# Two attention-plus-spectral layers: row sums directly behind a chunk's last product with V, and all range maxima of weights at chunk boundaries

## The chip, the cores and the metric

The kernel runs on one core of a Trainium2 chip. The metric is the device time of one execution in microseconds (us). A core has a TensorE (PE in the profile, PEld for its weight loads), a VectorE (DVE), a ScalarE (ACT), a GpSimd (POOL) and a SyncE (SP), which issues nearly all DMAs here. Each engine works off its own list of instructions in the listed order; an instruction that waits holds up everything listed behind it on the same engine.

## The reference

The input x is 2048 x 1024. Four residual blocks follow each other: attention, spectral filter, attention, spectral filter, both attentions with the same weights and both filters with the same weights.

```python
def _A_ref(x, wqkv, wo):          # 32 heads of 32
    q, k, v = split(x @ wqkv)
    p = softmax(q @ k.T * Dh ** -0.5)
    return (p @ v) @ wo
def _B_ref(x, w_r, w_i):
    return irfft2(rfft2(x) * (w_r + 1j * w_i))
x = x + _A_ref(_layernorm(x), A_wqkv, A_wo)
x = x + _B_ref(_layernorm(x), B_w_r, B_w_i)
x = x + _A_ref(_layernorm(x), A_wqkv, A_wo)
x = x + _B_ref(_layernorm(x), B_w_r, B_w_i)
```

## The kernel before, in words

"Layer one" is the first attention and the first filter (layer 0 in the code), "layer two" the second pair.

**Range flags.** The fast code represents float32 numbers as pairs of float16, which is exact enough only if the weights lie in a certain range. So the kernel also finds the largest absolute value of all weights, and at the very end `combine_flags` chooses whether a general fallback runs (it doesn't for these inputs). The maxima are VectorE reductions, all in layer one: 48 over the staged pieces of wqkv in `Weights.prep` (L259, 128x512 float32 each), 16 over the pieces of wo that `spectral` loads for that purpose alone (L789), and 32 over the spectral weights in `loadw` (L840). In layer two the same code runs with `flag`/`flags` None and without any of them.

**Start of a layer.** `ln` normalizes 16 tiles of 128 rows, splits each into high and low float16 halves `hl` (L168 on VectorE) and transposes them by DMA into `xh`, `xl` (the tile `big`). Between the tiles TensorE makes the first K, Q and V (L338, L382). `bank()` gives them the PSUM banks o and x in turn; `split` (L167 on ScalarE, L168 on VectorE) empties a bank.

**Attention.** 8 groups of 4 heads (g), each in 4 chunks of 512 queries (c), each in 16 steps of 128 keys (kt): 512 steps per layer. In a step TensorE makes the scores `S` (L564) into two of three PSUM buffers `s`, ScalarE takes the exponentials `p` (L568), and after every second step the products with V, `PV` (L574), follow for two steps together. VectorE adds the exponentials of the chunk into `acc` (`add`, L585 for the first two steps together, L587 for the others). Behind the last `add` of a chunk comes `fin`: four matmuls of `acc` with ones (L593) make the row sums, into an `s` buffer as well; VectorE transposes them (L594), inverts them (L596), spreads them (L599) and scales the chunk's output (L600). `out` writes it to DRAM a few steps later (L607, L609). Every odd step has a slot for "filler" matmuls: K, Q and V of coming groups (L338, L382) in groups 0 to 6, the output projection (L440) in group 7. K and Q fillers use the one x bank, which must be emptied before the next of them starts. `Weights.prep` splits the weights of a coming phase in such slots.

**Order.** In the attention loop the orders of TensorE and ScalarE are as the program is written (`manual_schedule`); those of VectorE, GpSimd and SP come from a list scheduler. In the loop before the change, step 0 of a chunk holds S, then the last two PVs of the chunk before and the add of its step 14; step 1 holds S, the add of step 15 and `fin`.

**Spectral filter.** `spectral` transforms along one axis (`t1`, `fa`), then runs a loop of 36 turns over 32 units (`fb`, `fc`, `binv`, `cinv`: transform, multiply with a weight tile `w` of `loadw`, transform back), then the last transform (`t2`, `ai`). In `loadw` GpSimd changes signs in the tile `w` (L848), behind the reduction of the same tile.

Of the kernel before, what the change touches and what calls it, by code (L numbers as in the profile page):

```python
# [6 lines left out]
F32 = mybir.dt.float32  # L7
# [5 lines left out]
ALU = mybir.AluOpType  # L13
AX = mybir.AxisListType
# [11 lines left out]
WOFF = np.cumsum([0] + [2 * 64 * len(u[2]) for u in UNITS]).tolist()  # L26
# [75 lines left out]
SW = 2.0 ** 8  # L102
# [86 lines left out]
class AttnPools:  # L189
# [22 lines left out]
    def open_small(self):  # L212
        small = self.small = Pools(self.tc, "left")
        self.pp = small("at_p", 8)
        self.qp = small("at_q", 1)
        self.oc = small("at_oc", 1)
        self.sgp = small("at_stage", 3)
        self.wqp = small("at_wqk", 2)
        self.wvp = small("at_wv", 1)
        self.sq = small("at_sq", 1)  # L220
        self.on = small("at_on", 2)
        self.on2 = small("at_on2", 2)
        self.sm = small("at_sm", 2)
        self.stages = [(self.sgp, "wst")] * 3 + [(self.on, "zt")] * 2 + [(self.on2, "ohl")] * 2


class Weights:


    def __init__(self, nc, ap, wp, flag):  # L230
        self.nc, self.ap, self.wp, self.flag, self.W, self.n = nc, ap, wp, flag, {}, 0

    def prep(self, ph):
# [22 lines left out]
        for i, (h, l, _) in enumerate(sl):  # L256
            split(nc, h, l, st[i], SW)
            if self.flag is not None:
                nc.vector.tensor_reduce(self.flag.pop(), st[i], axis=AX.XY, op=ALU.max, apply_absolute_value=True)  # L259
            load()  # L260
            yield


# [4 lines left out]
def attention(nc, tc, layer, ap, xin, yd, wts, wo, cst, dram, flags):  # L268
# [280 lines left out]
    run(prep(phases[0]))  # L549
    last_v = vk.pop()  # L550
    for v in vk:
        run(v)
# [28 lines left out]
    def add(g, c, kt):  # L581
        for hf in range(2):
            p = P[g, c, kt, hf]
            if kt == 1:
                nc.vector.scalar_tensor_tensor(acc[hf], P[g, c, 0, hf], 1e-34, p, op0=ALU.add, op1=ALU.add)  # L585
            elif kt:
                nc.vector.tensor_add(acc[hf], acc[hf], p)  # L587

# [45 lines left out]
    with tc.manual_schedule(engines={mybir.EngineType.PE, mybir.EngineType.Activation}):  # L634
        for g in range(NG):
# [3 lines left out]
            for u in range(NCH * NKT):  # L639
# [40 lines left out]
        for w in late + pend:  # L680
            add(*w)
        run(wof)
    with tc.manual_schedule(engines={mybir.EngineType.PE}):
        ps, xs, folds = [], [xres(3, t) for t in range(4)], fold_rests()
# [71 lines left out]
def spectral(nc, tc, ap, yd, xout, a, cst, fast, flags=None, nxt=None):  # L756
# [22 lines left out]
    xo = ap.x.rearrange("p t (a u g q) -> p g a t u q", a=8, g=2, q=8)  # L779
    wos = []  # L780

    def absmax(i):

        if flags is not None and 0 <= i < 16:
            s = p3.tile([128, 512], F32, name="wo")
            nc.sync.dma_start(s, a["wo"][(i // 2) * 128:(i // 2 + 1) * 128, (i % 2) * 512:(i % 2) * 512 + 512])
            wos.append(s)
        while len(wos) == 3 or (wos and i == 15):
            tc.keep_in_program_order(nc.vector.tensor_reduce(flags["wcol"].pop(), wos.pop(0), axis=AX.X, op=ALU.max, apply_absolute_value=True))  # L789

# [40 lines left out]
    def loadw(i):  # L831
# [294 lines left out]
def combine_flags(nc, tc, pool, flags, cst):  # L1126

    assert not flags["wcol"]
    f = pool.tile([128, 6], F32, name="f4")
    fw, fb = (pool.tile([128, 1], F32, name=n) for n in ("fwm", "fwbm"))  # L1130
    nc.vector.reduce_max(fw, flags["w"], axis=AX.X)
    nc.vector.reduce_max(fb, flags["wb"], axis=AX.X)
    v = pool.tile([128, 1], F32, name="fv")
# [29 lines left out]
def build(nc, tc, a):  # L1163
    with ExitStack() as ctx:
# [9 lines left out]
        for h in range(4):  # L1174
# [4 lines left out]
            "mv": cp.tile([128, 32, 2], F32, name="fmv"),  # L1179
            "w": cp.tile([128, 64], F32, name="fw"),  # L1180
            "wb": cp.tile([128, 32], F32, name="fwb"),
# [3 lines left out]
        flags["wcol"] = [flags["w"][:, i:i + 1] for i in range(64)]  # L1185
        nc.vector.memset(flags["r"], 0.0)
# [55 lines left out]
```

## Time and profile before

| what | us |
|---|---|
| median of 3 runs (lowest, highest) | 3838.1 (3837.2, 3840.4) |
| the profiled execution: its time, and the span of its instructions | 3841.8, 3839.8 |
| busy in the span: PE, DVE, ACT, POOL | 3713.6, 3165.3, 2900.6, 309.1 |
| layer one: first to last score matmul (L564) | 118.2 to 1622.0 |
| layer two: first to last score matmul (L564) | 2039.0 to 3524.0 |
| layer one: spectral loop, first L864 to first L967 | 1723.8 to 1886.2 |
| layer two: spectral loop, first L864 to first L967 | 3625.5 to 3776.2 |

Durations below are from the profiled execution. A row of a timeline gives the start, the duration, the engine, line, operation and tiles, the count where several are merged, and in brackets the idle time of the engine before it and what ended that. A row of groups gives count, busy time, mean time of one in ns, and the idle time before the group. A row of the list of waits gives the waiting engine and line, what it waited for, the total, the number and the longest. Since both layers run the same attention and filter code, and only layer one has the reductions, the two halves of one trace can be laid side by side.

### The profile page before, as it was taken

Reading aid. Unit: us, or ns where it says so; the run is one execution under the profiler, and the core shown is the slowest. Engines: PE = TensorE matmul, PEld = TensorE weight load, DVE = VectorE, ACT = ScalarE, POOL = GpSimd, SP = SyncE. Lnnn points to the kernel's source line nnn. Section 1 sums busy time; section 2 is a strip of 40 time slices with the busy share of each in tenths; the row PEclk is TensorE's granted clock in tenths of the full one; section 3 lists DMA queues with packets and bytes.
Section 4 is the critical chain, followed back from the end, with each engine's and each line's share of the span. In section 5 each row is a group of like instructions: output and inputs, shape, how many; then the busy total and the mean of one; then the engine's idle time right before and its main releaser. Section 6 shows DMA issues by size and latency. Waiting matters only on the chain.

```text
span 3839.8 us, 79585 instructions
## 1 busy us (share of the span) xinstructions
PE 3713.6 (97%) x32951; PEld 1637.3 (43%) x32951; DVE 3165.3 (82%) x3869; ACT 2900.6 (76%) x3567; POOL 309.1 (8%) x386
## 2 busy tenths in 40 slices
PE   6999999999999999999989999999999999999998
PEld 4422433342234233378854334333423432333788
DVE  6789899889998988965666998899899889889554
ACT  4687887888788876667856888888888888666595
POOL 1000000000000000004320000000000000000143
PEclk9999999999999999999999999999999999999999
DMA  8000000000000221244270000000000002112433
GB/s 206 15 18 18 12 12 18 18 12 16 14 26 7 72 67 70 72 147 135 63 176 15 18 18 13 12 18 23 10 18 12 23 12 91 53 64 72 151 99 105
DMA packets 165573, 194.07 MB, mean 51 GB/s; under 512 B 74960, under 2 KB 120656, under 8 KB 164176
## 3 DMA queue, kind: packets, MB, share of 16 engines
q1 hardware_dynamic: 164912, 188.82, 16.0%
q8 instruction: 260, 4.26, 0.5%
q14 instruction: 113, 0.93, 0.1%
q10 hardware_dynamic: 288, 0.07, 0.0%
HBM read 123.83 MB, written 48.23 MB: 45 GB/s over the span
## 4 chain that ended last, share of the span: by engine, by line
PE 74%; DVE 11%; issue 8%; ACT 3%; DMA 2%; POOL 2%; SPq 0%; DVEq 0%; POOLq 0%; ACTq 0%
PE o L574 20%; PE s L564 17%; PE x L338 12%; PE x L382 7%; PE x L440 6%; DVE R L587 3%; PE s L440 2%; PE ps L864 2%; PE ps L804 2%; ACT p L568 1%; PE s L593 1%; PE ps L795 1%; PE ps L979 1%; DMA wst<-in_wp 1%; PE ps L933 1%
## 5 line engine op out<-in xcount | busy, mean ns | idle before, releaser
L568 ACT ACTIVATE p<-s,bias 128x1024 f32<-128x1024 f32 x2048 | 2169.8, 1112 | 553.6 <-PE s L564 536.7
L587 DVE TENSOR_TENSOR R<-R,p 128x1024 f32<-128x1024 f32 x1792 | 2084.4, 1217 | 109.0 <-ACT p L568 105.7
L574 PE MATMUL o<-p,R 128*32 128x512 f32 x8192 | 985.2, 598 | 0.0
L338 PE MATMUL x<-big,wqk 128*128 128x512 f16 x2880 | 679.2, 381 | 16.8 <-DVE R L168 7.6
L564 PEld LDWEIGHTS <-R 32*128 32x128 f16 x12288 | 231.2, 92 | 755.3 <-issue 639.8
L338 PEld LDWEIGHTS <-wqk 128*128 128x128 f16 x3072 | 276.9, 98 | 449.7 <-issue 163.0
L574 PEld LDWEIGHTS o<-p,R 128*32 128x32 f32 x8192 | 213.7, 109 | 524.1 <-issue 524.1
L564 PE MATMUL s<-R 32*128 32x512 f16 x6144 | 430.2, 378 | 6.7 <-ACT p L568 5.0
L564 PE MATMUL s<-Q,R 32*128 32x512 f16 x6144 | 425.7, 378 | 7.1 <-DVE R L481 5.5
L382 PE MATMUL x<-wv,big 128*128 128x256 f16 x2784 | 331.9, 276 | 35.4 <-DMA big<-hl 35.4
L382 PEld LDWEIGHTS <-big 128*128 128x128 f16 x3072 | 293.1, 99 | 147.3 <-issue 68.9
L585 DVE SCALAR_TENSOR_TENSOR R<-p 128x1024 f32<-128x1024 f32 x128 | 153.8, 1203 | 197.2 <-ACT p L568 196.8
L440 PE MATMUL x<-big 128*128 128x512 f16 x1050 | 241.6, 380 | 0.0
L363 POOL PARTITION_ALL_REDUCE mall<-mqk x16 | 43.0, 2684 | 2310.6 <-DVE mqk L357 2299.1
L440 PEld LDWEIGHTS <-big 128*128 128x128 f16 x1344 | 124.3, 98 | 180.6 <-issue 42.7
L912 DVE TENSOR_TENSOR H<-G,H 128x512 f16<-128x512 f32 (+1 forms) x68 | 46.3, 680 | 113.7 <-ACT H L911 113.6
L864 PE MATMUL ps<-cbi,H 128*128 128x256 f16 (+1 forms) x792 | 100.2, 275 | 7.6 <-ACT H L911 6.0
L857 ACT COPY U<-ps 64x256 f32<-64x256 f32 (+1 forms) x272 | 97.2, 357 | 10.9 <-PE ps L864 5.8
L857 ACT COPY B<-ps 64x256 f32<-64x256 f32 (+1 forms) x272 | 97.1, 357 | 7.0 <-PE ps L864 3.5
L864 PE MATMUL ps<-cb,big 128*128 128x256 f16 x780 | 97.2, 274 | 0.0
L167 ACT ACTIVATE R<-x 128x512 f16<-128x512 f32 x88 | 52.6, 598 | 53.4 <-PE x L338 53.3
L864 PEld LDWEIGHTS <-H 128*128 128x128 f16 (+1 forms) x792 | 76.6, 99 | 20.2 <-ACT H L911 7.1
(428 smaller groups left out, 2922.8 us busy)
## 6 DMA issues: line engine op xcount, KB each, us to landing
wst<-in_wp SPq DMA_DIRECT2D x96, 256.0 KB, 3.0
R<-y SPq DMA_DIRECT2D x32, 512.0 KB, 5.3
w<-in_w SPq DMA_DIRECT2D x60, 256.0 KB, 2.7
od<-ohl SPq DMA_DIRECT2D x56, 256.0 KB, 2.4
big<-od SPq DMA_DIRECT2D x16, 896.0 KB, 6.9
y<-R SPq DMA_DIRECT2D x20, 512.0 KB, 2.6
R<-in_x SPq DMA_DIRECT2D x16, 512.0 KB, 5.5
wst<-in_wo SPq DMA_DIRECT2D x32, 256.0 KB, 3.1
```

The lines of the kernel that those rows point to most:

```text
L167: nc.scalar.activation(hi, src, AF.Copy, scale=scale)
L338: nc.tensor.matmul(ps, a, b, start=d == 0 and i == 0, stop=d == 7 and i == 2)
L382: nc.tensor.matmul(ps[:, j], l, r, start=d == 0 and i == 0, stop=d == 7 and i == 2)
L440: nc.tensor.matmul(p, a, b, start=start and d == ds[0] and i == 0, stop=stop and d == ds[-1] and i == 2)
L564: nc.tensor.matmul(s[h // 2][:, h % 2], K[g][r, a, kt * 128:kt * 128 + 128], Q[g][r, b, c * 512:c * 512 + 512], start=i == 0, stop=i == 2)
L568: nc.scalar.activation(p, s[hf], AF.Exp, bias=bias[g], scale=SCALE / (SQ * SQ))
L574: nc.tensor.matmul(O[g, c][32 * h:32 * h + 32], V[g][:, kt, 32 * h:32 * h + 32], P[g, c, kt, h // 2][:, h % 2], start=kt == 0, stop=kt == ...
L585: nc.vector.scalar_tensor_tensor(acc[hf], P[g, c, 0, hf], 1e-34, p, op0=ALU.add, op1=ALU.add)
L587: nc.vector.tensor_add(acc[hf], acc[hf], p)
L804: nc.tensor.matmul(pa[:, j], tt[:, j], mm[:, g], start=True, stop=True)
L857: nc.scalar.copy(ov[64 * r:64 * r + 64, a0:a0 + m, x], tl[64 * x:64 * x + 64, :m, r])
L864: nc.tensor.matmul(out, l, r, start=k == 0, stop=k == len(mm_) - 1)
```

## The change

1. **Row sums earlier.** In step 0 of a chunk, behind S and the last two PVs of the chunk before, both adds are now issued, then a maximum (`wts.look()`, tied behind the last add on VectorE), then `fin`. So the four matmuls with ones stand ahead of S of step 1 on TensorE. That holds for 31 boundaries of each layer; the end of the last chunk is as before.
2. **Maxima.** The reductions in `prep`, `absmax` and `loadw` are gone, and with `absmax` its 16 loads. Instead `look` reduces one piece of 128x1024. In layer one these are 24 pieces of the high halves in float16 that `prep` has made anyway (5 of them at the end of the start, 19 at boundaries). In layer two they are 17 pieces of the spectral weights and 8 of wo in float32, loaded for this by SP into two buffers `lookp` (512 KB each, asked for one boundary or more ahead), at 25 boundaries.
3. `combine_flags` joins three arrays of maxima instead of two. A reserved area for DMA descriptors is made smaller (`dynamic_dma_scratch_size=4096`), which makes room for the two buffers.

```diff
-            if self.flag is not None:
-                nc.vector.tensor_reduce(self.flag.pop(), st[i], axis=AX.XY, op=ALU.max, apply_absolute_value=True)
             load()
             yield
+        if self.flag is not None:
+            v = w[:, 0].rearrange("p d n -> p (d n)")
+            self.unseen += [(v[:, o:o + 1024], None) for o in range(0, 512 * len(sl), 1024)]
+
+    def take(self, i):
+        if len(self.unseen) > i and self.unseen[i][1] is not None:
+            src = self.unseen[i][1]
+            t = self.ap.lookp.tile([128, 1024], F32, name="look")[:, :src.shape[1]]
+            self.nc.sync.dma_start(t, src)
+            self.unseen[i] = (t, None)
+
+    def look(self):
+        if self.unseen:
+            self.take(0)
+            self.nc.vector.tensor_reduce(self.cols.pop(0), self.unseen.pop(0)[0], axis=AX.X, op=ALU.max,
+                                         apply_absolute_value=True)
+            self.take(0)
...
     last_v = vk.pop()
+    if layer == 0:
+        for _ in range(5):
+            wts.look()
...
                     late = pend
                     pend = []
+                    if kt == 0 and late:
+                        for w in late:
+                            last_add = add(*w)
+                        with tc.issue_after(last_add.ins):
+                            wts.look()
+                        done = [late[1][:2]]
+                        fin(*done[0])
+                        late = []
                 for w in late[:1]:
                     add(*w)
-                    if w[2] == NKT - 1:
-                        fin(*w[:2])
-                        done = [w[:2]]
...
-        if i % 2:
-            absmax(i // 2)
...
         nc.sync.dma_start(wt, a["w"][:, WOFF[i]:WOFF[i + 1]])
-        if flags is not None:
-            nc.vector.tensor_reduce(flags["wb"][:, i:i + 1], wt, axis=AX.X, op=ALU.max, apply_absolute_value=True)
...
-        wts = [Weights(nc, ap, a["wp"], None if layer else flags["wcol"]) for layer in range(2)]
+        later = [a["w"][:, o:min(o + 1024, WOFF[-1])] for o in range(0, WOFF[-1], 1024)]
+        later += [a["wo"][128 * d:128 * d + 128, :] for d in range(8)]
+        wts = [Weights(nc, ap, a["wp"], True, cols[0], []),
+               Weights(nc, ap, a["wp"], None, cols[1] + cols[2], [(None, v) for v in later])]
```

The order of TensorE at the first boundary of layer one, before (big, wqk: a filler's operands; R holds K, Q, V and acc; the eleven further pairs of a load and a score matmul are cut at the dots):

```order
L574 MATMUL o<-p,R 32x512 x8
L564 LDWEIGHTS R
L564 MATMUL s<-R 128x512
...
L593 MATMUL s<-R,ones 32x512 x4
L338 LDWEIGHTS wqk
L338 MATMUL x<-big,wqk 128x512
```

and after the change (L596 is PV, L616 the row sums, L586 S, L357 the filler):

```order
L596 MATMUL o<-p,R 32x512 x8
L616 MATMUL s<-R,ones 32x512 x4
L586 LDWEIGHTS R
L586 MATMUL s<-R 128x512
...
L357 LDWEIGHTS wqk
L357 MATMUL x<-big,wqk 128x512
```

The row sums have moved from behind the twelve score matmuls of step 1 to ahead of them.

The order of VectorE at the third boundary of layer two, before (p: exponentials; zt, rc, fr: the row sums on their way; x: the filler's bank; sq: squares of the K or Q just emptied):

```order
L587 TENSOR_TENSOR R<-R,p 128x1024 x6
L585 SCALAR_TENSOR_TENSOR R<-p 128x1024
L594 STREAM_TRANSPOSE zt<-s 128x512
L585 SCALAR_TENSOR_TENSOR R<-p 128x1024
L596 RECIPROCAL rc<-zt 128x16
L168 SCALAR_TENSOR_TENSOR R<-x,R 128x512
L597 TENSOR_TENSOR fr<-fr,rc 128x16
L599 STREAM_TRANSPOSE zt<-rc 128x512
L342 TENSOR_TENSOR sq<-R 128x512
L600 SCALAR_TENSOR_TENSOR zt<-oc,zt 128x512
L587 TENSOR_TENSOR R<-R,p 128x1024 x8
```

and after:

```order
L609 TENSOR_TENSOR R<-R,p 128x1024 x6
L278 TENSOR_REDUCE fwb<-look 128x1
L617 STREAM_TRANSPOSE zt<-s 128x512
L619 RECIPROCAL rc<-zt 128x16
L620 TENSOR_TENSOR fr<-fr,rc 128x16
L622 STREAM_TRANSPOSE zt<-rc 128x512
L623 SCALAR_TENSOR_TENSOR zt<-oc,zt 128x512
L607 SCALAR_TENSOR_TENSOR R<-p 128x1024 x2
L168 SCALAR_TENSOR_TENSOR R<-x,R 128x512
L361 TENSOR_TENSOR sq<-R 128x512
L609 TENSOR_TENSOR R<-R,p 128x1024 x8
```

The maximum and the whole work on the row sums now stand ahead of the next chunk's first two adds, and the emptying of the x bank stands behind these.

The order of VectorE towards the end of layer one's start, before (hl: low halves of a normalized tile; R<-o and R<-x: banks being emptied; wst: staged weights):

```order
L168 SCALAR_TENSOR_TENSOR hl<-xn,hl 128x1024 x2
L168 SCALAR_TENSOR_TENSOR R<-o,R 128x512
L259 TENSOR_REDUCE fw<-wst 128x1
L168 SCALAR_TENSOR_TENSOR hl<-xn,hl 128x1024
L259 TENSOR_REDUCE fw<-wst 128x1
L168 SCALAR_TENSOR_TENSOR R<-x,R 128x512
L259 TENSOR_REDUCE fw<-wst 128x1
L168 SCALAR_TENSOR_TENSOR R<-x,R 128x512
L168 SCALAR_TENSOR_TENSOR R<-o,R 128x512 x2
```

and after:

```order
L168 SCALAR_TENSOR_TENSOR hl<-xn,hl 128x1024 x2
L168 SCALAR_TENSOR_TENSOR R<-o,R 128x512
L168 SCALAR_TENSOR_TENSOR hl<-xn,hl 128x1024 x2
L168 SCALAR_TENSOR_TENSOR R<-x,R 128x512 x2
L168 SCALAR_TENSOR_TENSOR R<-o,R 128x512 x2
```

The three reductions of staged weights that stood between the emptying of the banks are gone. In layer one's spectral loop VectorE's order after the change is, row for row, that of layer two.

More of the change, by code (lines that the diff above doesn't have):

```diff
@@ L586, in add @@
             elif kt:
-                nc.vector.tensor_add(acc[hf], acc[hf], p)
+                last_add = nc.vector.tensor_add(acc[hf], acc[hf], p)
+        return last_add if kt > 1 else None
     def fin(g, c):
@@ L682, in attention @@
         run(wof)
+    assert not wts.unseen and not wts.cols
     with tc.manual_schedule(engines={mybir.EngineType.PE}):
@@ L1126, in combine_flags @@
 def combine_flags(nc, tc, pool, flags, cst):
-    assert not flags["wcol"]
     f = pool.tile([128, 6], F32, name="f4")
-    fw, fb = (pool.tile([128, 1], F32, name=n) for n in ("fwm", "fwbm"))
-    nc.vector.reduce_max(fw, flags["w"], axis=AX.X)
-    nc.vector.reduce_max(fb, flags["wb"], axis=AX.X)
+    fw, fb, fo = (pool.tile([128, 1], F32, name=n) for n in ("fwm", "fwbm", "fwom"))
+    for m, n in ((fw, "w"), (fb, "wb"), (fo, "wo")):
+        nc.vector.reduce_max(m, flags[n], axis=AX.X)
+    nc.vector.scalar_tensor_tensor(fw, fw, 1.0 / SW, fo, op0=ALU.mult, op1=ALU.max)
     v = pool.tile([128, 1], F32, name="fv")
@@ L1184, in build @@
         }
-        flags["wcol"] = [flags["w"][:, i:i + 1] for i in range(64)]
         nc.vector.memset(flags["r"], 0.0)
```

20 lines of the change are left out of this document (8 added, 12 removed).

## The prediction

> **What bounds the kernel now.** I read the chain of waits first, then compared the two layers, which run the same code except for the reductions.
>
> ```profile
> PE 74%; DVE 11%; issue 8%; ACT 3%; DMA 2%; POOL 2%; SPq 0%; DVEq 0%; POOLq 0%; ACTq 0%
> 118.20:1622.00 1503.80, 427.53 (x6140) 115.73 (x6144) 1.00 0.08 28
> 2039.00:3524.00 1485.00, 427.67 (x6144) 115.45 (x6144) 1.00 0.09 28
> ```
>
> The chain is TensorE's, with VectorE second. The two windows reach from the first to the last score matmul of a layer: 1503.8 us in layer one, 1485.0 in layer two. So the attention that carries the reductions is 18.8 us longer. The list of waits in groups 0 to 6 says how; layer one, then layer two, TensorE's waits over 1.5 us in total, with one of VectorE on top:
>
> ```profile
> DVE fw L259 <- DMA wst<-in_wp: 7.8, 10, 2.3
> PE x L338 <- DVE Q L168: 6.2, 4, 2.3
> PE s L355 <- DVE sq L342: 5.1, 3, 1.9
> PE x L338 <- DVE R L168: 3.2, 3, 2.2
> PE s L593 <- DVE R L587: 2.2, 2, 1.7
> PE s L564 <- ACT p L568: 1.9, 3, 1.2
> ```
> ```profile
> PE s L564 <- ACT p L568: 3.1, 2, 1.7
> PE s L355 <- DVE sq L342: 2.4, 3, 1.0
> PE s L564 <- DVE mqk L357: 1.9, 7, 0.3
> ```
>
> 18.6 us against 7.4. Layer two is near TensorE's own pace; layer one waits for VectorE. One case in layer one's timeline, and below it twelve of the same matmuls in layer two:
>
> ```profile
> 286.70 1.32 DVE L259 TENSOR_REDUCE fw<-wst 128x1 f32<-128x512 f32 x2 [1.96 <-DMA wst<-in_wp]
> 295.48 4.32 PE L338 MATMUL x<-big,wqk 128*128 128x512 f16 x12 [2.21 <-DVE R L168]
> ```
> ```profile
> 2217.84 2.76 PE L338 MATMUL x<-big,wqk 128*128 128x512 f16 x12
> ```
>
> VectorE loses 1.96 us waiting for a staged piece and 1.32 reducing it; nine microseconds later the x bank is emptied late, TensorE stands for 2.21, and the twelve matmuls behind take 4.32 instead of 2.76: 1.56 more, at a slower pace. So a wait costs more than its length.
>
> VectorE is nevertheless not short of time:
>
> ```profile
> L585 DVE SCALAR_TENSOR_TENSOR R<-p 128x1024 f32<-128x1024 f32 x128 | 153.8, 1203 | 197.2 <-ACT p L568 196.8 <-PE s L593 0.3
> ```
>
> It idles 197.2 us ahead of the first add of the chunks, at some 62 boundaries 3 us each.
>
> **The change part by part.**
>
> *Reductions out of layer one's attention.* 40 of the 48 lie in the loop. Their removal makes the VectorE work between boundaries that of layer two: 18.8 us by the windows. Bounds: 18.6 - 7.4 = 11.2 if only the named waits go; 18.8 + 7.4 = 26 if layer two's own waits could go as well. I take 18.8, since everything else is alike.
>
> *Reductions out of the start.*
>
> ```profile
> 77.34 0.69 DVE L259 TENSOR_REDUCE fw<-wst 128x1 f32<-128x512 f32 x1 [4.49 <-DMA wst<-in_wp]
> 78.68 6.70 PE L338 MATMUL x<-big,wqk 128*128 128x512 f16 x24 [4.35 <-DVE R L168]
> 32.60:118.20 85.60, 77.91 (x486) 48.15 (x487) 41.10 (x83) 34.90 (x44) 13.73 (x13) 0.95 0.62 131
> 1961.40:2039.00 77.60, 74.25 (x490) 46.94 (x488) 28.87 (x62) 30.20 (x42) 12.31 (x12) 1.00 0.70 152
> ```
>
> A reduction waits 4.49 us for the weights of the next phase; behind it in the list stands the emptying of the x bank, and TensorE waits 4.35 for that. The 24 matmuls then take 6.70 where twice the twelve above would take 5.5: 1.2 more. Together 5.6. The two windows hold the same matmuls of the start in both layers (granted clock 0.95 against 1.00): 85.6 against 77.6, so at most 8.0. At least 0, if the transposes of the same stretch take over. I take 5.6. The Trainium skill (TensorE: Matmul & The Clock Gate, the section on the HAM clock gate) has the clock halved after an idle window of about 3.4 us and full again after a busy one; by that the 4.35 us gap would cost up to 1.7 more and the 2.21 us gap nothing. The 1.56 us behind the shorter gap disagrees; by the page the sum would be 0.5 us larger here and the attention's unchanged.
>
> *Reductions out of the spectral loop.* Layer one, then layer two (PE, PEld, DVE, ACT, POOL busy, granted clock, DMA):
>
> ```profile
> 1723.80:1886.20 162.40, 152.63 (x1303) 136.19 (x1303) 94.76 (x231) 132.31 (x340) 70.44 (x102) 0.99 0.34 106
> 3625.50:3776.20 150.70, 147.05 (x1302) 134.19 (x1302) 74.44 (x190) 130.41 (x340) 70.12 (x102) 1.00 0.36 113
> ```
>
> The same matmuls, 41 fewer VectorE instructions, 162.4 - 150.7 = 11.7 us less. VectorE's order in layer one becomes that of layer two, so I take 11.7; at least 6.1, the difference of TensorE's idle time (9.8 against 3.7). The 16 reductions of wo lie mostly in the stretch before and gain nothing.
>
> *Boundary.* The third of layer two:
>
> ```profile
> 2173.86 2.36 DVE L587 TENSOR_TENSOR R<-R,p 128x1024 f32<-128x1024 f32 x2 [0.25 <-ACT p L568]
> 2179.07 1.23 DVE L585 SCALAR_TENSOR_TENSOR R<-p 128x1024 f32<-128x1024 f32 x1 [2.85 <-ACT p L568]
> 2180.21 0.71 DVE L594 STREAM_TRANSPOSE zt<-s 128x512 f32<-128x512 f32 x1
> 2180.84 1.18 DVE L585 SCALAR_TENSOR_TENSOR R<-p 128x1024 f32<-128x1024 f32 x1
> 2181.95 0.24 DVE L596 RECIPROCAL rc<-zt 128x16 f32<-128x16 f32 x1
> 2182.11 0.63 DVE L168 SCALAR_TENSOR_TENSOR R<-x,R 128x512 f16<-128x512 f32 x1
> 2182.65 0.16 DVE L597 TENSOR_TENSOR fr<-fr,rc 128x16 f32<-128x16 f32 x1
> 2182.73 0.70 DVE L599 STREAM_TRANSPOSE zt<-rc 128x512 f32<-128x512 f32 x1
> 2183.36 0.38 DVE L342 TENSOR_TENSOR sq<-R 128x512 bf16<-128x512 f16 x1
> 2183.66 0.68 DVE L600 SCALAR_TENSOR_TENSOR zt<-oc,zt 128x512 f32<-128x512 f32 x1
> 2184.26 2.35 DVE L587 TENSOR_TENSOR R<-R,p 128x1024 f32<-128x1024 f32 x2
> ```
> ```profile
> 2175.20 1.93 PE L574 MATMUL o<-p,R 128*32 128x512 f32 x16
> 2177.06 0.83 PE L564 MATMUL s<-R 32*128 32x512 f16 x12
> 2177.81 1.07 PE L593 MATMUL s<-R,ones 128*32 128x512 f32 x8
> 2178.81 1.90 PE L338 MATMUL x<-big,wqk 128*128 128x512 f16 x8
> 2184.02 2.33 PE L338 MATMUL x<-big,wqk 128*128 128x512 f16 x10
> ```
>
> The adds end at 2176.22, so the row sums can follow PV at 2177.0 and end at 2178.1. The maximum costs between 0.69 (the 128x512 reduction, if float16 goes twice as fast) and 1.2 (the 128x1024 add's 1203 ns); I take 1.2, twice the elements of 0.69: it ends at 2177.4, covered by the row sums. Then L594 to L600 take 0.71 + 0.24 + 0.16 + 0.70 + 0.68 = 2.49, to 2180.6; the exponentials of step 1, 1.0 later than 2179.07, are there by 2180.1. Two L585: 2183.0; L168 ends at 2183.6, L342 at 2184.0. The next adds start at 2184.0 instead of 2184.26, so VectorE hides the maximum. The x bank is emptied at 2183.6 instead of 2182.74, and its filler comes at 2184.02: hidden with 0.4 to spare; without that cover a boundary would cost 0.8. TensorE does the same matmuls. PV's 16 passes take 1.86 from start to start and the row sums' 8 take 1.00, 0.07 more than half: switching, which joining the two may save, 62 x 0.07 = 4.3 at most. Against it stands the boundary with the latest adds:
>
> ```profile
> 2083.43 3.48 DVE L587 TENSOR_TENSOR R<-R,p 128x1024 f32<-128x1024 f32 x3
> 2085.09 1.92 PE L574 MATMUL o<-p,R 128*32 128x512 f32 x16
> ```
>
> Adds end at 2086.91, PV's feed at 2086.95: no wait to speak of. I take a gain of 2, with bounds of 4.3 and, at 0.1 us each, -6.
>
> *Loads.* The 25 transfers of 512 KB in layer two are asked for a boundary or more ahead of their use, and what stands behind them on SP's queue (weight pieces, outputs of a chunk) is needed only in a later chunk: zero. If one came late, VectorE would wait at the maximum and the row sums' transposes behind it, at up to the 4.49 us of the late weights above. The smaller area for descriptors has no price: no row shows it in use.
>
> Sum: 18.8 + 5.6 + 11.7 + 2 = 38. The profiled execution took 3841.8 (span 3839.8), 3.7 above the median of the runs; I take the gain off the median: 3838.1 - 38 = **3800**.
>
> **Rivals.**
>
> *Half of it.* The start's transposes take the reductions' place (0), the attention returns only the named waits (11.2), the spectral loop 6.1, and boundaries cost 2: 15 us, 3823. For it: late VectorE work has several causes. Against it: layer two shows the full amounts.
>
> *Work counts, not its place.* 40 x 0.69 = 27.6 us of VectorE work cost 18.8, so 0.68 per us. The 19 and 25 maxima of 1.2 at boundaries are 22.8 and 30 us, costing 15.5 and 20.4: attention loses 17.1, start and spectral loop win 17.3: 3838, no change (3832 if layer one's go at 0.69). Against it: the idle 197.2 us. The Trainium skill (VectorE: DVE Perf Modes, the perf-mode tier table) lists the reduction at 1x for every type, so float16 would save nothing and 3838 would be this rival's time; no reduction of float16 is in this trace.
>
> *The row sums hold up TensorE: slower.* They stand ahead of S of step 1, so if the last add is late, S, its exponentials and all fillers wait. The row above has a 1.7 us wait of L593 for L587, in layer one with VectorE loaded. It turns into a loss from 38 / 62 = 0.6 us a boundary; at 1.0 the time is 3838 + 62 - 38 = 3862. Against it: without reductions the adds end with PV or before, as at 2086.91.
>
> **How the numbers follow.** Forecast 0.77, half 0.12, no change 0.06, slower 0.05. A difference under 0.2% (7.7 us) can't be told from none here. Faster: the first two and a little of the third, 0.90; same 0.05; slower 0.05. The range is 3788 (the attention's and boundary's upper bounds in good part) to 3820, into the half case.
>
> **What would show it.** The two L564 windows near 1485 each; the first score matmul near 112 instead of 118.2; 150 to 152 us in layer one's spectral loop; L585 with about a third of its idle time; no growth of L593's waits. I would be wrong if L593 or L338 waited for VectorE at boundaries, or if layer two's window grew by more than 5 us.

## The result and the profile after

The changed kernel takes 3792.2 us (median of 4 runs, 3789.6 to 3796.2), the kernel before beside it 3839.0 (4 runs): a ratio of 0.9879, 95% interval 0.9862 to 0.9896, 46.8 us less. The profiled executions stand 52.2 apart (3841.8 and 3789.6): that of before lies above all four of its runs, that of the changed kernel is the fastest of its four.

In the changed kernel the lines have moved: scores L586 (before L564), exponentials L590 (L568), products with V L596 (L574), row sums L616 (L593), first add L607 (L585), adds L609 (L587), transposes L617 and L622 (L594, L599), Q and K beside the scores L357 (L338), their squares L361 (L342), norms L374 (L355). A look is L278.

The chain of waits, and from the costliest groups the first add of a chunk and the transpose of the row sums:

```profile
PE 85%; DVE 6%; issue 4%; ACT 2%; DMA 1%; POOL 1%; SPq 0%; DVEq 0%; POOLq 0%; ACTq 0%
...
L607 DVE SCALAR_TENSOR_TENSOR R<-p 128x1024 f32<-128x1024 f32 x128 | 150.7, 1218 | 34.6 <-ACT p L590 34.6
...
L617 DVE STREAM_TRANSPOSE zt<-s 128x512 f32<-128x512 f32 x64 | 45.7, 714 | 62.8 <-PE s L616 62.7
```

TensorE holds 85% of the chain instead of 74%, VectorE 6% instead of 11. The first adds idled 197.2 us; the 34.6 left are two waits of 17.3, one at the start of each layer, so the hole ahead of the first adds is gone. What idle time VectorE still has at the boundaries lies ahead of L617, about 1 us for each of 64.

Windows from the first to the last score matmul of layer one and of layer two, then the spectral loop of layer one and of layer two (us; busy PE, PEld, DVE, ACT, POOL; granted clock, DMA):

```profile
111.40:1591.30 1479.90, 1471.20 (x13637) 515.83 (x13636) 1354.96 (x1409) 1179.48 (x1246) 33.77 (x31) 1.00 0.08 28
1994.20:3473.50 1479.30, 1471.03 (x13637) 515.64 (x13636) 1361.74 (x1421) 1179.60 (x1246) 34.60 (x31) 1.00 0.11 36
1693.40:1845.70 152.30, 147.68 (x1302) 134.47 (x1302) 75.04 (x190) 130.48 (x340) 70.20 (x102) 1.00 0.36 118
3575.10:3725.70 150.60, 146.66 (x1302) 133.96 (x1300) 74.80 (x190) 130.15 (x340) 70.17 (x102) 1.00 0.35 113
```

The two attentions are now equal. Where the 52.1 us between the two spans went, from these windows and those of before:

| stretch | before | after | difference |
|---|---|---|---|
| start to the first score matmul | 118.2 | 111.4 | -6.8 |
| layer one's attention | 1503.8 | 1479.9 | -23.9 |
| from there to its spectral loop | 101.8 | 102.1 | +0.3 |
| layer one's spectral loop | 162.4 | 152.3 | -10.1 |
| from there to layer two's first score matmul | 152.8 | 148.5 | -4.3 |
| layer two's attention | 1485.0 | 1479.3 | -5.7 |
| from there to the end | 315.8 | 314.2 | -1.6 |

Two profiles of the same code differ as well. In the runs below, four profiles with layer one's attention unchanged give it 1499.6 to 1503.8 us, and six with layer two's unchanged give that 1484.8 to 1487.9. So a difference of two windows is uncertain by 3 to 4 us.

The third boundary of layer two in the timeline, VectorE and then TensorE:

```profile
2128.37 2.36 DVE L609 TENSOR_TENSOR R<-R,p 128x1024 f32<-128x1024 f32 x2 [0.24 <-ACT p L590]
2130.65 1.21 DVE L278 TENSOR_REDUCE fwb<-look 128x1 f32<-128x1024 f32 x1
2132.56 0.72 DVE L617 STREAM_TRANSPOSE zt<-s 128x512 f32<-128x512 f32 x1 [0.70 <-PE s L616]
...
2134.50 0.69 DVE L623 SCALAR_TENSOR_TENSOR zt<-oc,zt 128x512 f32<-128x512 f32 x1
2135.11 2.35 DVE L607 SCALAR_TENSOR_TENSOR R<-p 128x1024 f32<-128x1024 f32 x2
2137.38 0.68 DVE L168 SCALAR_TENSOR_TENSOR R<-x,R 128x512 f16<-128x512 f32 x1
```
```profile
2129.71 1.92 PE L596 MATMUL o<-p,R 128*32 128x512 f32 x16
2131.45 1.04 PE L616 MATMUL s<-R,ones 128*32 128x512 f32 x8
2132.43 0.83 PE L586 MATMUL s<-R 32*128 32x512 f16 x12
2133.19 1.90 PE L357 MATMUL x<-big,wqk 128*128 128x512 f16 x8
...
2138.39 2.76 PE L357 MATMUL x<-big,wqk 128*128 128x512 f16 x12
```

The look ends at 2131.86, the transposes wait 0.70 for the row sums all the same, and the x bank, emptied at 2138.06, is there 0.33 before its filler: the working of the prediction, nearly to the tenth. TensorE needs 2133.19 - 2129.71 = 3.48 us from the products to the filler, where before it needed 2178.81 - 2175.20 = 3.61 with the same matmuls. Over the 31 boundaries of layer two the median of this stretch falls from 3.61 to 3.47 us and the mean from 3.69 to 3.58.

### The profile page after: what moved, and what is told of

Read it like the earlier page. It is cut to its first block, busy times and chain, and to the rows that moved or that the text cites. A ratio compares the mean times of both kernels' runs of the same rounds, so it can differ in the third digit from the quotient of the medians.

```text
span 3787.7 us, 79598 instructions
## 1 busy us (share of the span) xinstructions
PE 3694.6 (98%) x32951; PEld 1640.7 (43%) x32951; DVE 3179.3 (84%) x3824; ACT 2893.2 (76%) x3567; POOL 308.2 (8%) x386
## 3 DMA queue, kind: packets, MB, share of 16 engines
q8 instruction: 260, 4.26, 0.5%
## 4 chain that ended last, share of the span: by engine, by line
PE 85%; DVE 6%; issue 4%; ACT 2%; DMA 1%; POOL 1%; SPq 0%; DVEq 0%; POOLq 0%; ACTq 0%
PE o L596 23%; PE s L586 19%; PE x L357 15%; PE x L401 7%; PE x L459 6%; PE ps L879 3%; PE s L459 2%; DVE R L609 2%; PE ps L823 2%; PE s L616 2%; PE ps L948 1%; PE ps L911 1%; PE ps L814 1%; PE ps L994 1%; PE ps L982 1%
## 5 line engine op out<-in xcount | busy, mean ns | idle before, releaser
L590 ACT ACTIVATE p<-s,bias 128x1024 f32<-128x1024 f32 x2048 | 2168.7, 1112 | 569.1 <-PE s L586 553.2
L609 DVE TENSOR_TENSOR R<-R,p 128x1024 f32<-128x1024 f32 x1792 | 2087.2, 1218 | 130.9 <-ACT p L590 127.6
L596 PE MATMUL o<-p,R 128*32 128x512 f32 x8192 | 985.0, 598 | 0.0
L357 PE MATMUL x<-big,wqk 128*128 128x512 f16 x2880 | 676.4, 380 | 1.7 <-ACT R L405 0.9
L586 PEld LDWEIGHTS <-R 32*128 32x128 f16 x12288 | 230.7, 92 | 752.9 <-issue 636.8
L357 PEld LDWEIGHTS <-wqk 128*128 128x128 f16 x3072 | 275.7, 98 | 419.6 <-issue 131.3
L596 PEld LDWEIGHTS o<-p,R 128*32 128x32 f32 x8192 | 213.7, 109 | 523.3 <-issue 523.3
L586 PE MATMUL s<-R 32*128 32x512 f16 x6144 | 430.2, 378 | 5.2 <-ACT p L590 3.3
L586 PE MATMUL s<-Q,R 32*128 32x512 f16 x6144 | 427.3, 377 | 4.6 <-DVE R L500 2.6
L607 DVE SCALAR_TENSOR_TENSOR R<-p 128x1024 f32<-128x1024 f32 x128 | 150.7, 1218 | 34.6 <-ACT p L590 34.6
L617 DVE STREAM_TRANSPOSE zt<-s 128x512 f32<-128x512 f32 x64 | 45.7, 714 | 62.8 <-PE s L616 62.7
L828 DVE TENSOR_TENSOR big<-ps,big 128x512 f16<-128x512 f32 x64 | 44.5, 695 | 57.8 <-ACT big L827 57.8
```

The costliest lines, as they stand in the source:

```text
L357: nc.tensor.matmul(ps, a, b, start=d == 0 and i == 0, stop=d == 7 and i == 2)
L586: nc.tensor.matmul(s[h // 2][:, h % 2], K[g][r, a, kt * 128:kt * 128 + 128], Q[g][r, b, c * 512:c * 512 + 512], start=i == 0, stop=i == 2)
L590: nc.scalar.activation(p, s[hf], AF.Exp, bias=bias[g], scale=SCALE / (SQ * SQ))
L596: nc.tensor.matmul(O[g, c][32 * h:32 * h + 32], V[g][:, kt, 32 * h:32 * h + 32], P[g, c, kt, h // 2][:, h % 2], start=kt == 0, stop=kt == ...
L609: last_add = nc.vector.tensor_add(acc[hf], acc[hf], p)
```

## The experiments

All runs are compared with runs of the kernel before on the same chip; "window" is that from first to last score matmul. Where maxima are not taken, their array is preset at the start.

### One part of the change at a time

**The new order at the boundary alone**, all reductions kept:

```diff
+                    if kt == 0 and late:
+                        for w in late:
+                            add(*w)
+                        done = [late[1][:2]]
+                        fin(*done[0])
+                        late = []
                 for w in late[:1]:
                     add(*w)
-                    if w[2] == NKT - 1:
-                        fin(*w[:2])
-                        done = [w[:2]]
```

> The kernel before with the new order at the chunk boundary alone: both last adds, then the row sums directly behind the last product with V. All reductions stay where they were and no look is added. Theory A (the boundary was undersized: the joined row sums leave out one change from float32 to float16 matmuls, 0.11 us each, and the adds and banks behind come earlier): about 11 us faster, 5 to 6 in the attention window of each layer, so near 3828. Theory B (as predicted, a boundary is worth 2 us in all, and the rest of the surplus is the spread between executions): 2 us, 3837. Theory C (the new order only pays where the reductions are gone, since in layer one the last add is late): layer two 5 to 6 us shorter, layer one not shorter or longer, 3833 to 3845.

Measured: 3838.9 against 3842.8, ratio 0.9988 (0.9979 to 0.9997). The windows of both layers, and the waits of TensorE in layer one that bear on it:

```profile
120.60:1623.90 1503.30, 1480.53 (x13637) 517.12 (x13636) 1355.46 (x1424) 1179.56 (x1246) 28.01 (x31) 1.00 0.08 28
2041.20:3522.40 1481.20, 1472.54 (x13637) 516.50 (x13636) 1333.44 (x1389) 1179.16 (x1246) 29.22 (x31) 1.00 0.08 28
```
```profile
PE s L355 <- DVE sq L342: 5.9, 3, 2.1
PE x L338 <- DVE Q L168: 4.8, 4, 2.0
...
PE s L593 <- DVE R L587: 2.6, 3, 1.1
PE s L593 <- DVE R L481: 1.4, 1, 1.4
```

Layer two is 3.8 us shorter, layer one 0.5: theory C, with less in layer two than its 5 to 6. From the products to the filler, layer two's boundaries take 3.58 us in the mean instead of 3.69, layer one's 3.88 instead of 3.90. Where VectorE carries the reductions, what TensorE saves at a boundary it waits for again, in part for the last adds (L593 for L587, 2.6 us).

**The 40 weight reductions of layer one's loop left out:**

```diff
-            if self.flag is not None:
+            if self.flag is not None and ph in PH0:
                 nc.vector.tensor_reduce(self.flag.pop(), st[i], axis=AX.XY, op=ALU.max, apply_absolute_value=True)
```

> The kernel before with the 40 weight reductions in layer one's loop left out (these maxima are not taken; the 8 of the start stay). Theory A (their place and their waits for staged weights cost what the two windows differ by): layer one's window falls from 1503.8 to 1485 to 1486, 18 to 19 us faster, 3820. Theory B (only the named waits go): 11 us, 3828, and waits of TensorE for other VectorE work appear. Theory C (VectorE work costs 0.68 us for each us wherever it stands): 27.6 x 0.68 = 18.8, the same as A; the run with the maxima in mid-chunk tells these two apart.

Measured: 3819.2 against 3842.8, 0.9936 (0.9922 to 0.9949). Layer one's window:

```profile
113.50:1598.60 1485.10, 1473.73 (x13637) 512.08 (x13636) 1323.67 (x1389) 1181.67 (x1246) 34.76 (x31) 1.00 0.08 28
```

1485.1, 18.7 less than in the profile of before and 14.5 less than the shortest window with these reductions: theory A's window, and theory B is out. Theory C forecasts the same number; the runs with the looks, below, decide against it. A further 4.7 came at the start, whose first score matmul moved from 118.2 to 113.5. That I had not expected of this run: the reductions of the loop's first phase are issued in the start.

**The 8 reductions of the start left out** (the condition above with `not in`):

> The kernel before with the 8 weight reductions of layer one's start left out (these maxima are not taken). Theory A (the wait of one reduction for the next phase's weights holds up the emptying of a bank): first score matmul near 112 instead of 118.2, 5.6 to 6.8 us faster, 3832. Theory B (transposes or loads take over as the bound of the start): under 2 us, 3837. Theory C (0.68 us for each us of VectorE work): 8 x 0.69 x 0.68 = 3.8 us, 3834.

Measured: 3839.3 against 3842.8, 0.9994 (0.9985 to 1.0003): not told apart from nothing. The first score matmul comes at 114.4. A wait of 4.35 us for L168 has become one of 3.83, still behind a reduction of the next phase (L259 on VectorE; the emptying of the bank stands two places behind it):

```profile
67.08 0.69 DVE L259 TENSOR_REDUCE fw<-wst 128x1 f32<-128x512 f32 x1 [4.55 <-DMA wst<-in_wp]
69.55 6.82 PE L382 MATMUL o<-wv,big 128*128 128x256 f16 x48 [3.83 <-DVE R L168]
76.20 5.34 PE L338 MATMUL x<-big,wqk 128*128 128x512 f16 x24
```

So the price of the start is shared by two sets of reductions; either taken alone gives 3.8 or 4.7, both together 6.8.

**The 32 reductions of w in the spectral loop left out:**

```diff
-        if flags is not None:
-            nc.vector.tensor_reduce(flags["wb"][:, i:i + 1], wt, axis=AX.X, op=ALU.max, apply_absolute_value=True)
```

> The kernel before with the 32 reductions of w in layer one's spectral loop left out (these maxima are not taken; the 16 of wo stay). Theory A (the loop becomes layer two's): 162.4 us fall to 151 to 152, 10 to 12 us faster, 3827, and the stretch behind it as in the changed kernel another 2 to 4. Theory B (only TensorE's idle time in the loop goes): 6 us, 3832.

Measured: 3832.1 against 3842.8, 0.9974 (0.9961 to 0.9987). The loop takes 152.7 us, 9.7 less: nearer theory A than B. TensorE's idle time in it falls from 9.8 to 4.4 us, and its busy time from 152.6 to 148.3 with the same matmuls:

```profile
1724.50:1877.20 152.70, 148.34 (x1303) 135.57 (x1301) 77.02 (x196) 130.65 (x340) 69.91 (x102) 0.98 0.35 113
```

Of the 2 to 4 us behind the loop 1.0 came with it (151.8 instead of 152.8 to layer two's first score matmul).

### The wait for the transfer, or the work

**The reductions kept, each behind the lower half of its own piece's split:**

```diff
-            split(nc, h, l, st[i], SW)
+            lo = split(nc, h, l, st[i], SW)
             if self.flag is not None:
-                nc.vector.tensor_reduce(self.flag.pop(), st[i], ...)
+                with self.ap.tc.issue_after(lo.ins):
+                    nc.vector.tensor_reduce(self.flag.pop(), st[i], ...)
```

> The kernel before with all 48 weight reductions kept, each held behind the VectorE half of the same piece's split, which comes when the piece has long been there, so that no reduction waits for a transfer. Theory A (part of the 18.7 us was the wait for a transfer, part the 0.69 us of work in mid-chunk, at the 0.37 to 0.49 us for each us that the looks in mid-chunk cost): the 27.6 us of work still cost 10 to 14, layer one's window falls to 1495 to 1499, 5 to 9 us faster than before, and the start 4 more. Theory B (the transfers' waits were the whole cost): layer one's window near 1486, 18 us faster or more. Theory C (the waits cost nothing, the work does): window 1504, the same time.

Measured: 3827.4 against 3841.3, 0.9966 (0.9952 to 0.9979). First score matmul at 111.6, and the window:

```profile
111.60:1603.90 1492.30, 1475.98 (x13633) 513.29 (x13636) 1345.23 (x1427) 1181.85 (x1246) 35.19 (x31) 1.00 0.08 28
```

Between A and B, and nearer A. In these profiles, of the 18.7 us 11.5 were the place behind a transfer (1503.8 - 1492.3) and 7.2 the work (1492.3 - 1485.1), 0.26 for each of its 27.6 us. The split is rough: against the shortest window of before, 1499.6, the first part is 7.3, and the whole kernel gained 13.9 us, of which 6.6 are the start's. That both parts exist is shown, their sizes only to some 4 us. At the start the waits were everything: 111.6 with all reductions, 111.4 in the changed kernel.

### What the looks cost, and where

**The changed kernel again:**

> The changed kernel once more, beside the kernel before on one chip, with more runs. Theory A (the gain is the mechanism's): ratio 0.986 to 0.990, and the profile again with layer one's window at 1480 and layer two's at 1479. Theory B (the surplus over the predicted 38 us came from a slow profiled run of before and a fast one of the changed kernel): 38 to 42 us, ratio 0.989 to 0.990.

Measured: 3791.9 against 3840.5, 0.9871 (0.9856 to 0.9886); its profiled execution, 3796.0, has windows of 1480.1 and 1479.8. Theory A.

**No looks:**

```diff
-            self.take(0)
-            self.nc.vector.tensor_reduce(self.cols.pop(0), self.unseen.pop(0)[0], ...)
-            self.take(0)
+            self.cols.pop(0), self.unseen.pop(0)
```

> The changed kernel with none of its 49 looks, and without the 25 loads for them (no range maximum of a weight is taken). Theory A (the looks lie in VectorE's idle time behind the last add): the same within 3 us, both windows at 1479 to 1480. Theory B (VectorE work costs 0.68 us for each us wherever it stands): 44 looks x 1.21 x 0.68 = 36 us faster. Theory C (only the 25 loads of layer two cost, on SP's queue): layer two's window 2 to 5 us shorter, layer one's the same.

Measured: 3792.0, ratio 0.9872 (0.9857 to 0.9887), on the chip of the run above. Windows:

```profile
110.80:1589.70 1478.90, 1471.26 (x13638) 515.66 (x13636) 1333.87 (x1389) 1180.52 (x1246) 34.51 (x31) 1.00 0.08 28
1996.80:3475.70 1478.90, 1470.84 (x13633) 515.47 (x13636) 1333.85 (x1389) 1180.54 (x1246) 34.79 (x31) 1.00 0.08 28
```

VectorE has some 21 and 28 us less to do and the time is the same: theory A. In the windows the looks and the 25 loads cost 1.2 and 0.9 us at most (1480.1 and 1479.8 in the run above), no more than profiles differ by themselves. Outside them this run loses 2.1 us for another reason (last section).

**The looks in mid-chunk**, behind the add of step 7:

```diff
-                        with tc.issue_after(last_add.ins):
-                            wts.look()
...
                 for w in late[:1]:
-                    add(*w)
+                    last_add = add(*w)
+                    if kt == 8 and (g or c):
+                        with tc.issue_after(last_add.ins):
+                            wts.look()
```

> The changed kernel with each look behind the add of step 7 in step 8 of a chunk, not behind the last add at the boundary. Theory A (what cost time in layer one was the wait for staged weights inside VectorE's order; a look has none, its data lie ready): within 5 us of the changed kernel. Theory B (the place is what counts: in mid-chunk VectorE has no slack, and 1.21 us more make the emptying of a bank late): 0.47 us for each of 44, the price of a reduction in the loop before (18.7 / 40), or more for the longer look: 20 to 36 us slower than the changed kernel.

Measured: 3816.2, 0.9939 (0.9925 to 0.9952), 24.3 us slower than the changed kernel beside it, 0.55 a look. Both windows, and a look with what follows it, VectorE and then TensorE:

```profile
111.80:1600.50 1488.70, 1477.71 (x13637) 516.15 (x13636) 1353.05 (x1409) 1179.58 (x1246) 35.17 (x31) 1.00 0.08 28
2003.30:3498.00 1494.70, 1477.52 (x13637) 516.27 (x13636) 1359.49 (x1421) 1179.41 (x1246) 34.05 (x31) 1.00 0.11 36
```
```profile
2116.94 1.22 DVE L278 TENSOR_REDUCE fwb<-look 128x1 f32<-128x1024 f32 x1
2118.07 2.35 DVE L609 TENSOR_TENSOR R<-R,p 128x1024 f32<-128x1024 f32 x2
2120.34 0.69 DVE L168 SCALAR_TENSOR_TENSOR Q<-x,Q 128x512 f16<-128x512 f32 x1
```
```profile
2121.08 2.75 PE L357 MATMUL x<-big,wqk 128*128 128x512 f16 x12 [0.67 <-DVE Q L168]
```

Theory B. The same instruction that is free at the boundary makes the emptying of a bank late here, with no transfer to wait for.

**Every look twice:**

```diff
-            self.nc.vector.tensor_reduce(self.cols.pop(0), self.unseen.pop(0)[0], ...)
+            col, (src, _) = self.cols.pop(0), self.unseen.pop(0)
+            for _ in range(2):
+                self.nc.vector.tensor_reduce(col, src, ...)
```

> The changed kernel with every look done twice, 1.21 us more at 44 boundaries. Theory A (the cover is the 1.0 us in which VectorE waits for the row sums, and the next bank has 0.3 to 0.4 us to spare): the transposes start 0.5 later, the bank comes 0.1 to 0.2 late at the boundaries with a filler there; 5 to 20 us slower. Theory B (there is cover to spare): within 3 us. Theory C (each late bank also slows the matmuls behind it, as the 1.56 us behind a gap of 2.21 did): 20 to 60 us slower.

Measured: 3802.0, 0.9902 (0.9887 to 0.9917): 10.1 us slower than the changed kernel. Its windows are 2.6 us longer in layer one (1482.7 instead of 1480.1) and 8.4 in layer two (1488.2 instead of 1479.8). Theory A. TensorE's largest wait in layer two is the one that the prediction had covered with 0.4 to spare (L358 is the changed kernel's L357):

```profile
PE x L358 <- DVE R L168: 5.2, 6, 1.3
```

### What the order at the boundary is worth

**The changed kernel with the row sums back behind the scores of step 1:**

```diff
-                    if kt == 0 and late:
...
                 for w in late[:1]:
-                    add(*w)
+                    last_add = add(*w)
+                    if w[2] == NKT - 1:
+                        with tc.issue_after(last_add.ins):
+                            wts.look()
+                        fin(*w[:2])
+                        done = [w[:2]]
```

> The changed kernel with the row sums back behind the scores of step 1, as before the change; the looks stay, behind the last add. Theory A (the new order is worth one change from float32 to float16 matmuls per boundary, 3.5 us a layer, and up to 2 of small waits): windows of 1483 to 1486, 7 to 11 us slower than the changed kernel. Theory B (in the old order a look makes the transposes and the next bank late, and the new order is what makes room for it): 20 us slower or more, with waits of TensorE for L168 at the boundaries. Theory C (the order is worth what was predicted): 2 us.

Measured: 3802.3 against 3842.9, 0.9901 (0.9886 to 0.9916); the changed kernel had 0.9871 on another chip, so 0.30% or 11.5 us. The intervals of the two ratios touch, so the windows are the better witness:

```profile
110.50:1594.90 1484.40, 1473.89 (x13637) 512.00 (x13636) 1345.19 (x1409) 1181.98 (x1246) 33.69 (x31) 1.00 0.08 28
1998.00:3482.60 1484.60, 1473.77 (x13637) 512.24 (x13636) 1351.82 (x1421) 1181.68 (x1246) 35.03 (x31) 1.00 0.11 36
```

4.3 and 4.8 us more than in the second profile of the changed kernel: about 5 us a layer, theory A. TensorE never waits for L168 at a boundary here, which speaks against B.

**Products with V in groups of four steps:**

```diff
-        self.pp = small("at_p", 8)
-        self.lookp = small("at_look", 2)
+        self.pp = small("at_p", 10)
+        self.lookp = small("at_look", 1)
...
-                if kt % 2 == 0:
+                if kt % 4 == 0:
                     for w in pend:
                         PV(*w)
-                    late = pend
                     pend = []
+                if kt % 2 == 0:
+                    late, fresh = fresh, []
```

> The changed kernel with the products with V in groups of four steps, not of two: half as many changes from float32 matmuls with V back to float16 ones; ten buffers for the exponentials in place of eight, one for the loads of the looks in place of two. Theory A (each visit left out saves what joining the row sums saved, 0.525 + 0.304 - 0.409 - 0.307 = 0.113 us): 128 visits a layer, 14.5 us a layer, 29 us faster than the changed kernel. Theory B (a burst of 7.4 us of products leaves ScalarE without scores, and the exponentials fall behind): TensorE waits for the exponentials, 0 to 60 us slower. Theory C (the saving at the boundary came from the adds being earlier, not from the change of type): within 3 us.

Measured: 4078.7 against 3842.9, 1.0615 (1.0601 to 1.0630): theory B, and far beyond its price. The largest wait of TensorE and the largest of ScalarE in layer one:

```profile
PE s L586 <- ACT p L590: 129.8, 122, 2.0
```
```profile
ACT p L590 <- PE s L586: 370.2, 275, 3.3
```

During a burst of products ScalarE gets no scores; behind it TensorE waits for exponentials, 122 times about 1 us. The saving of theory A can't be seen under that, so it is not shown for other places than the boundary.

**The smaller descriptor area alone**, in the kernel before:

```diff
-    nc = _bacc.Bacc("TRN2", target_bir_lowering=False, num_devices=1)
+    nc = _bacc.Bacc("TRN2", target_bir_lowering=False, num_devices=1, dynamic_dma_scratch_size=4096)
```

> The kernel before with nothing but the smaller area for DMA descriptors. Theory A (it does nothing): the same within 2 us. Theory B (the 1.6 us that the changed kernel is shorter behind its last matmul, and the 2 us behind each spectral loop, come from it): 2 to 6 us faster, with 62.0 in place of 63.6 us from layer two's last stage to the end.

Measured: 3842.0 against 3842.9, 0.9996 (0.9987 to 1.0005), and 63.5 us from layer two's first L967 to the end, with 63.6 before: theory A.

No version here beats the changed kernel.

## Why the prediction was right, and which term was mis-sized

- **What bounds the kernel.** Right: layer two's pace was near TensorE's own, and layer one came down to it.
- **Reductions out of layer one's attention, 18.8.** Measured 18.7 by themselves, with the uncertainty of a window. The reason given was half the story: "a wait costs more than its length" fits the waits (11.5 us of window for 7.8 us of VectorE's waits for staged weights; at the low end of the spread, 7.3, it would not), but some 7 us were plain work in a place without slack.
- **Reductions out of the start, 5.6.** Measured 6.8. The wait of 4.35 us that was found belongs to the reductions of the next phase: without them TensorE waits no more for L168 there, and 4.7 us are saved. Without the start's own reductions the same kind of wait comes some 9 us earlier, 3.83 long. The 2.1 us from 4.7 to 6.8 lie within the spread of the start, 109.8 to 112.4 us in the versions of the changed kernel.
- **Reductions out of the spectral loop, 11.7.** Measured 9.7 alone and 10.1 in the changed kernel. Layer two's loop itself lies between 149.8 and 153.5 in the profiles taken, so 150.7 was one draw of that.
- **The boundary, 2, and at most 4.3.** The step that failed. The changed kernel's order is worth 5.2 us in layer one (1485.1 without the loop's reductions against 1479.9) and 5.7 in layer two, some 11 in all, beyond the bound. It holds in every pair of profiles: in windows without the weight reductions the old order takes 1484.4 us or longer here, the new one with at most one look a boundary 1481.2 or shorter (groups of four and looks in mid-chunk left aside). That is at least 3.2 a layer. The saving was sized as the row sums' 1.00 less half of the products' 1.86. But those 1.86 held the switch to the score matmuls too, at their end. The right comparison is from the products to the filler, 3.61 before and 3.48 after: 0.13 a boundary, 62 x 0.13 = 8 at most; by the means of layer two 0.11, or 3.4 us a layer. The trace of before shows the switch itself: four such float32 passes take 0.43 us from start to start where more of them follow, and 0.545 where float16 matmuls follow. Whether the type makes it or the other tile of the array (`128*32` against `32*128` or `128*128`) stays open; the `128*128` float32 matmuls of the spectral filter, 0.447 for four, take no longer ahead of float16. In layer two the order alone gave 3.8 of the 5.7; the rest fits a wait of 1.79 us for the exponentials, with slower matmuls behind it (last section), which that run still had and which is 1.06 in the changed kernel.
- **The terms were added as if they were independent.** They are not: the order alone gives nearly nothing in layer one while the reductions are there. As point values from the times of whole kernels, 23.6 (loop and its part of the start), 3.5, 10.7 and, with the reductions gone, 11.5 for the order make 49.3, against 46.8 and 48.6 measured for the whole.
- **The look hidden behind the row sums.** Right, at the upper end of its price (1.21 us) and free. The 0.4 us to spare was right as well: of a second 1.21, the 0.70 of waiting for the row sums and the 0.33 ahead of the filler leave 0.18 a boundary, and 10.1 / 44 = 0.23 was measured. The 0.8 named for cover that is gone was not tested.
- **Rival "work counts, not its place".** It falls: next to nothing at the boundary, 24.3 / (44 x 1.21) = 0.46 for each us in mid-chunk, one rate for each place and not 0.68 for all. Of its two times for a look the longer is right, 1.21 us in float32 and in float16:

```profile
L278 DVE TENSOR_REDUCE fwb<-look 128x1 f32<-128x1024 f32 x16 | 19.4, 1212 | 0.0
L278 DVE TENSOR_REDUCE fw<-wqk 128x1 f32<-128x1024 f16 x16 | 19.3, 1208 | 0.0
```

The Trainium skill (VectorE: DVE Perf Modes, the perf-mode tier table) has the reduction at 1x in its bf16 and in its float32 column; these rows, in float16 and float32, show one rate as well.

- **Rivals "half of it" and "row sums hold up TensorE".** The first falls with 18.7, 6.8 and about 10. The second does not occur in the changed kernel: its row sums wait there once a layer, and for L500, which empties an `s` buffer of the output projection, not for an add of exponentials:

```profile
PE s L616 <- DVE R L500: 1.4, 1, 1.4
```

The run with the order alone shows a trace of that rival, 2.6 us of L593's waits for the last adds in layer one, where the kernel before has 2.2: too little to lose by.
- **The signs named.** The windows came out 5 us below the 1485 that was named, the first score matmul and the loop (111.4 and 152.3) close to theirs. The idle time of the first adds fell to 34.6 us, under a fifth and not a third; 62.8 us of it now lie ahead of L617.
- **Not foreseen:** 4.3 us between layer one's spectral loop and layer two's scores, 2.1 of it explained below, the rest with a wait of TensorE for ScalarE that fell from 2.8 to 0.6 us; it is 1.4 to 2.8 in the versions of before and 1.8 in the second profile of the changed kernel, so part of that is spread. The 1.6 us at the end lie wholly behind the last instruction of VectorE (10.7 us from there to the end before, 9.0 after), where no work of the change stands. Their cause stays open; the kernel with the reductions behind the split had them too (61.9 us from layer two's first L967 to the end instead of 63.6), and the smaller descriptor area alone had not. That these 5.9 us came on top is luck: nothing in the working stands for them.

## What to carry to other kernels

Price extra work on a side engine by its place, not by its length: look for the point where that engine waits for the bound engine in every round, put the work there, on data that have already landed, and check with the doubled work how much cover is left. When two tasks of a type are joined, measure the whole stretch from before the first to behind the last in the trace of before, since a row's own length already holds the switch to what follows it. Take the terms of a sum away one by one and also all but one: two terms that share an engine's slack don't add.

## What the hardware showed that I had not expected

**VectorE stood still beside GpSimd.** At the end of layer one's spectral filter a float16 split of weights, 0.68 us elsewhere, takes 3.14. VectorE and GpSimd in the kernel before:

```profile
1911.77 3.14 DVE L168 SCALAR_TENSOR_TENSOR wqk<-wst,wqk 128x512 f16<-128x512 f32 x1
1914.84 0.68 DVE L990 TENSOR_TENSOR R<-R,ps 128x512 f32<-128x512 f32 x1
```
```profile
1911.33 3.03 POOL L994 TENSOR_TENSOR R<-R,sd 128x1024 f32<-128x1024 f32 x1 [4.82 <-DVE sd L989]
```

The split waits until GpSimd is done and then runs at its own pace; the add behind it, which reads PSUM, runs at 0.68 beside GpSimd in other places of the same list. In the kernel before three splits meet such an addition of GpSimd's; in the changed kernel two do, since the third has ended 0.7 us ahead of it (1870.17 and 1870.84), and the stretch from the end of the spectral loop to the last matmul of L979 takes 49.4 us instead of 51.5. The changed kernel without looks has three again, and 51.5; all other versions of the changed kernel here have two and the short stretch, all versions of the kernel before the long one. So 2.1 us of the gain come from a meeting that the change has moved without aiming at it. The Trainium skill (SBUF — State Buffer, the section on SBUF's two separate sides) says it so: a VectorE instruction with two inputs in SBUF and a GpSimd instruction that reads SBUF share a port pair, and the second of them stands still until the first has ended. These rows agree.

**The slower matmuls come behind some gaps only.** The prediction took 1.56 us of slower matmuls behind a gap of 2.21 for a price of waiting. In the run with the order alone a gap of 1.79 has them too, 4.26 us for twelve instead of 2.76; in the kernel before, a longer one, of 2.29, has not:

```profile
3241.59 0.96 PE L564 MATMUL s<-R 32*128 32x512 f16 x10 [1.79 <-ACT p L568]
3242.48 4.26 PE L338 MATMUL x<-big,wqk 128*128 128x512 f16 x12
```
```profile
236.39 2.75 PE L338 MATMUL x<-big,wqk 128*128 128x512 f16 x12 [2.29 <-DVE Q L168]
```

Over all these profiles the matmuls of Q and K ran slower in 19 places, the longest gap close ahead being 1.76 to 4.5 us; 4 to 11 of them took about 0.43 us each instead of 0.216, which cost 0.8 to 2.2 us. The Trainium skill (TensorE: Matmul & The Clock Gate, the section on the HAM clock gate) has the clock halved after an idle window of about 3.4 us, and that window running freely: the halved pace and its chance agree with these rows, the length doesn't, since 1.79 us were enough.
